# Local and strided attention scores packed into shared PSUM pairs, with batch 2's q and k transposed by DMA, in a fused attention and ELU-MLP kernel

## The chip, the cores and the metric

The kernel runs on one core of one Trainium2 chip. The metric is the device time of one execution in microseconds. TensorE (PE) multiplies, ScalarE (ACT) and VectorE (DVE) work element by element, GpSimd (POOL) here makes masks and issues most loads, and SyncE (SP) issues output stores and DMA transposes.

## The reference

Eight batches of eight heads, sequences of 576 tokens, head size 64. In heads 0 to 3 a query sees the last 32 keys (local); in heads 4 to 7 it sees earlier keys with the same position modulo 32 (strided). The result, with the heads side by side, goes through an MLP with ELU.

```python
scores = scale * np.matmul(q, k.transpose(0, 1, 3, 2))
rel = pos[:, None] - pos[None, :]
mask_local = (rel >= 0) & (rel < stride)
mask_strided = (rel >= 0) & (pos[None, :] % stride == pos[:, None] % stride)
...
attn = np.exp(scores)
attn = attn / (np.sum(attn, axis=-1, keepdims=True) + 1e-09)
return np.matmul(attn, v).astype(np.float32)
...
x = np.ascontiguousarray(attn_out.transpose(0, 2, 1, 3)).reshape(B * S, H * D)   # 4608 x 512
h = x @ w_in                                                                      # 2048 wide
g = np.where(h > 0.0, h, alpha * (np.exp(np.minimum(h, 0.0)) - 1.0))
return (g @ w_out).astype(np.float32)
```

## The kernel before, in words

Everything is one stream of tokens in the string `ORDER`, written out beforehand. The loop at the end of the kernel splits each token at its dots and calls one function; each engine then executes its instructions in the order in which the tokens issued them. A token's last field is the PSUM bank, or the banks, that it writes; there are eight banks, held as one tile `ps`, and 128 partitions.

Tokens are stored with the sequence split modulo 8 (`NS`): 72 (`RS`) positions in each of 8 residues. A strided score block is 72 by 72, because keys and queries of one residue modulo 8 meet; its mask `mask_s` does the rest. A local block takes 128 keys and 96 queries. A pair such as `2s0` or `2l1` means batch 2, strided or local heads, half 0 or 1: two heads. Each pair is worked in two units, 0 and 1.

For a batch the steps are:

- `D` loads q, k, v (`qs`, `ks`, `vs` strided; `ql`, `kl`, `vl` local), `w_in` (`wi`, `wj`) and `w_out` (`wo`). All of these are issued by GpSimd, which converts to bf16 on the way. `X` is a DMA transpose from a raw tile into `qT` or `kT`, issued by SyncE. Batches below `NPE` (3 before: batches 0, 1 and 2) have no `X`; they are transposed by TensorE with `T` (lines 418 and 421) and copied out of PSUM with `c` (VectorE) or `C` (ScalarE). For these batches `ql` and `kl` are loaded as runs of 512 bf16 columns; from `NPE` on in four loads of 64-column pieces, one for each head (L238, L245), with a second small load for `vl` (L257).
- `S` makes scores (L464): a strided unit is eight matmuls of 64 x 128 on 72 columns, a local unit six on 96 columns. Two heads are stored in two banks, 288 (`W`) columns in each. `e` is the exp on ScalarE (L471), `m` the mask product on VectorE (L478 strided, L484 local).
- `O` multiplies by the values (L527, L534; in batches 0 and 1, `OLDPV`, L491 to L512), with the sums of the softmax as extra columns. `n` takes the logarithm of the sums and `r` the exp of its negative on ScalarE (L562, L568); `x` writes the normalized result into `xT` on VectorE (L593).
- `W` and `V` copy v into its padded form on VectorE.

The MLP runs over nine chunks of 512 tokens. `L` (or, in chunk 0, `a` for two of the four row blocks and `b` for the others) is one of 16 hidden tiles: four matmuls of 128 x 128 on 512 columns (L623). `h` is the exp on ScalarE (L631), `i` a clamp on VectorE (L640) or `j` the same on ScalarE (L638), `g` the maximum with the tile in PSUM on VectorE (L651, L649). `Z` is a quarter of an output tile: four matmuls (L657). `o` (ScalarE) or `q` (VectorE) copies an output tile out of PSUM (L663), `t` stores it through SyncE's queue (L675). A chunk can start only when all batches that its 512 tokens touch are written into `xT`. The last output tile is made in two halves (`Y`, `y`).

Before `ORDER` starts, the program issues batch 0's q and k for the first strided heads through SyncE's and ScalarE's queues, then fills constants and issues the other loads of batch 0 on GpSimd. Raw tiles for q, k and v exist once (batch 1 uses free room in `xT` and `g`), so a load for a later batch waits until the transposes of the batch before have read the tile.

Of the kernel before, what the change touches and what calls it, by code (L numbers as in the profile page):

```python
# [9 lines left out]
BF16 = mybir.dt.bfloat16  # L10
I32 = mybir.dt.int32
ALU = mybir.AluOpType
# [3 lines left out]
S = 576  # L16
# [14 lines left out]
NPE = 3  # L31
OLDPV = (0, 1)


ORDER = """
w.7.28 F.k1 F.vs k.k.0 k.q.0 T.0s0.k.0.0 F.ms C.0s0.k.0 T.0s0.q.1.0 K.q.1 k.k.1 c.0s0.q.0
T.0s0.k.0.1 S.0s0.0.12 c.0s0.k.1 T.0s0.q.3.1 e.0s0.0 c.0s0.q.1 S.0s0.1.67 m.0s0.0 T.0s1.q.0 e.0s0.1
O.0s0.0.12 c.0s1.q m.0s0.1 T.0s1.k.7 n.0s0.0 F.ml D.wi0.0 O.0s0.1.56 r.0s0.0 c.0s1.k x.0s0.0 D.wj0.0
n.0s0.1 S.0s1.0.34 r.0s0.1 T.0l0.q.7 D.wi1.0 e.0s1.0 x.0s0.1 S.0s1.1.01 c.0l0.q T.0l0.k.2 e.0s1.1
D.wi2.0 m.0s1.0 c.0l0.k O.0s1.0.67 D.wi3.0 m.0s1.1 n.0s1.0 S.0l0.0.01 S.0l0.1.23 D.qs.1 V.0.0  # L40
e.0l0.0 O.0s1.1.45 e.0l0.1 D.ks.1 m.0l0.0 T.0l1.k.0 r.0s1.0 m.0l0.1 O.0l0.0.23 n.0s1.1 x.0s1.0
D.vs.1 T.0l1.q.1 r.0s1.1 c.0l1.k O.0l0.1.67 n.0l0.0 r.0l0.0 c.0l1.q n.0l0.1 V.0.1 D.ql.1 S.0l1.1.01
x.0l0.0 r.0l0.1 x.0s1.1 e.0l1.1 S.0l1.0.23 x.0l0.1 a.0.0.4 e.0l1.0 m.0l1.1 D.kl.1 O.0l1.1.67 m.0l1.0
O.0l1.0.23 n.0l1.1 r.0l1.1 a.0.2.5 n.0l1.0 x.0l1.1 a.0.1.0 r.0l1.0 D.vl.1 x.0l1.0 a.0.4.6 b.0.4
b.0.0 h.0.4 b.0.2 h.0.0 i.0.4 a.0.5.7 D.wo0.0 h.0.2 a.0.6.3 i.0.0 g.0.4 b.0.6 j.0.2 b.0.5 g.0.0
h.0.6 a.0.11.6 h.0.5 g.0.2 b.0.11 j.0.6 a.0.8.4 i.0.5 D.wo1.0 h.0.11 b.0.1 g.0.5 a.0.9.5 h.0.1 g.0.6
b.0.8 j.0.11 D.wo2.0 i.0.1 b.0.9 h.0.8 g.0.1 a.0.7.7 h.0.9 a.0.14.3 i.0.8 T.1s0.q.0 g.0.11 j.0.9
D.wo3.0 b.0.7 g.0.8 T.1s1.q.2 h.0.7 a.0.3.6 c.1s1.q T.1s0.k.1 C.1s0.q a.0.15.4 g.0.9 D.qs.2 C.1s0.k
T.1s1.k.2 i.0.7 b.0.15 c.1s1.k S.1s0.1.01 h.0.15 g.0.7 b.0.3 D.ks.2 e.1s0.1 b.0.14 i.0.15 h.0.3
g.0.15 T.1l1.q.7 S.1s0.0.01 h.0.14 m.1s0.1 S.1s1.0.45 D.ql.2 e.1s0.0 i.0.3 a.0.12.2 i.0.14 b.0.12  # L50
e.1s1.0 m.1s0.0 T.1l0.q.0 g.0.14 h.0.12 T.1l0.k.1 O.1s0.0.45 D.kl.2 C.1l0.q m.1s1.0 a.0.10.3 i.0.12
n.1s0.0 g.0.3 T.1l1.k.0 r.1s0.0 b.0.10 C.1l1.k x.1s0.0 a.0.13.6 g.0.12 h.0.10 O.1s0.1.45 C.1l0.k
c.1l1.q b.0.13 D.vs.2 V.1 n.1s0.1 S.1l1.0.12 h.0.13 Z.0.2.0.7 i.0.10 e.1l1.0 g.0.10 Z.0.1.0.0
r.1s0.1 m.1l1.0 j.0.13 x.1s0.1 S.1l0.1.12 g.0.13 O.1l1.0.34 D.vl.2 e.1l0.1 Z.0.2.1.7 n.1l1.0 m.1l0.1
r.1l1.0 Z.0.1.1.0 x.1l1.0 S.1l0.0.12 S.1s1.1.34 S.1l1.1.56 e.1l0.0 Z.0.2.2.7 e.1l1.1 m.1l0.0
Z.0.1.2.0 e.1s1.1 m.1l1.1 O.1l1.1.56 O.1l0.0.34 n.1l1.1 O.1s1.0.12 n.1l0.0 Z.0.2.3.7 m.1s1.1 n.1s1.0
r.1l0.0 r.1l1.1 Z.0.1.3.0 x.1l0.0 o.0.2 x.1l1.1 r.1s1.0 Z.0.0.0.3 t.0.2 o.0.1 x.1s1.0 Z.0.0.1.3
t.0.1 Z.0.0.2.3 Z.0.0.3.3 O.1s1.1.12 o.0.0 O.1l0.1.67 n.1s1.1 T.2s1.q.0 t.0.0 T.2s1.k.3 n.1l0.1
c.2s1.q r.1s1.1 T.2l0.k.5 c.2s1.k T.2l0.q.4 r.1l0.1 T.2l1.k.0 x.1s1.1 C.2l0.k T.2l1.q.3 x.1l0.1
S.2s1.0.12 C.2l1.k W.2 T.2s0.q.5 L.1.13.6 e.2s1.0 D.qs.3 c.2s0.q C.2l1.q c.2l0.q T.2s0.k.7 m.2s1.0  # L60
L.1.6.5 h.1.13 D.ks.3 V.2 j.1.13 c.2s0.k L.1.11.4 D.vs.3 h.1.6 g.1.13 D.ql.3 S.2s0.0.23 i.1.6 h.1.11
S.2l0.1.01 L.1.10.6 g.1.6 e.2s0.0 X.qs.3 i.1.11 e.2l0.1 L.1.8.7 m.2s0.0 h.1.10 g.1.11 O.2s0.0.01
h.1.8 L.1.5.2 m.2l0.1 i.1.10 n.2s0.0 i.1.8 O.2s1.0.34 X.ks.3 Z.0.3.0.5 g.1.10 r.2s0.0 g.1.8 h.1.5
Z.0.3.1.5 x.2s0.0 n.2s1.0 L.1.4.7 r.2s1.0 i.1.5 D.kl.3 g.1.5 L.1.7.6 h.1.4 x.2s1.0 Z.0.3.2.5 h.1.7
i.1.4 L.1.1.4 i.1.7 g.1.4 L.1.0.3 g.1.7 h.1.1 i.1.1 L.1.12.7 h.1.0 g.1.1 D.vl.3 X.ql.3 L.1.2.6 i.1.0
h.1.12 g.1.0 L.1.14.4 h.1.2 i.1.12 g.1.12 j.1.2 L.1.15.3 D.qs.4 h.1.14 g.1.2 L.1.3.7 h.1.15 i.1.14
# [86 lines left out]
def kernel(  # L153
# [157 lines left out]
    load_runs("vs", 0, 0, 2)  # L311
    load_runs("qs", 0, 2, 2)
    load_runs("ks", 0, 2, 2)
    load_runs("vs", 0, 2, 2)

    two = 1.00193786621093750

# [433 lines left out]
```

## Time and profile before

| what | value |
|---|---|
| runs | 310.74, 312.59, 312.9 us; median 312.59 |
| span of the profiled execution, first to last instruction | 309.4 us |
| its own time beside the span | not on the page; only the span is |
| TensorE busy | 297.2 us, 96%, 2374 matmuls recorded |
| VectorE, ScalarE busy | 223.4 us (72%), 233.7 us (76%) |
| GpSimd busy | 74.8 us (24%) |
| mean granted TensorE clock | 0.977 |
| DMA | 36.29 MB in 96952 packets |

The busy time of TensorE is the union of its matmuls, whose ends are modelled; a matmul's record is longer than its distance to the next one, so distances are read from start to start. Some matmul records are missing, so a count in the timeline can be one or two too low.

### The profile page before, as it was taken

What the parts mean: (1) busy time and instruction counts of PE and PEld (TensorE: products, weight loads), DVE (VectorE), ACT (ScalarE), POOL (GpSimd) and SP (SyncE); (2) the same over time, 40 slices, a digit from 0 to 9 for tenths busy, and PEclk for the clock granted to TensorE, in tenths of its full rate; (3) what the DMA queues carried; (4) which work ended last, traced back from release to release, by engine and by line L of the source; (5) the groups of instructions that cost most, each with busy time, mean ns of one, the idle gap of its engine ahead of it and who ended that gap; (6) DMA issues with size and microseconds to landing.
All of it is one profiled execution on the core that took longest, in us unless ns stands there. A gap on an engine that the chain in (4) does not pass through costs nothing.

```text
span 309.4 us, 6379 instructions
## 1 busy us (share of the span) xinstructions
PE 297.2 (96%) x2374; PEld 151.6 (49%) x2412; DVE 223.4 (72%) x445; ACT 233.7 (76%) x410; POOL 74.8 (24%) x104
## 2 busy tenths in 40 slices
PE   5989999999999999999999999999999999999994
PEld 5754545544554455444544544455444544444443
DVE  6869972999669976898689679946798359990100
ACT  4769976979887899887998997879886767881211
POOL 8933310761084048003810082000000000000000
PEclk9559999999999999999999999999999999999999
DMA  8999999999999999994999589222200220002222
GB/s 161 189 206 206 195 206 213 165 133 152 151 200 161 123 201 183 106 125 87 190 155 122 119 113 159 47 67 71 68 3 0 70 68 1 0 2 57 67 79 70
DMA packets 96952, 36.29 MB, mean 117 GB/s; under 512 B 77754, under 2 KB 92442, under 8 KB 96922
## 3 DMA queue, kind: packets, MB, share of 16 engines
q0 software_dynamic: 64608, 19.40, 61.0%
q1 hardware_dynamic: 31878, 16.09, 28.9%
q10 hardware_dynamic: 436, 0.40, 0.5%
q8 instruction: 19, 0.31, 0.4%
q14 instruction: 11, 0.09, 0.1%
HBM read 39.41 MB, written 9.44 MB: 158 GB/s over the span
## 4 chain that ended last, share of the span: by engine, by line
PE 72%; DVE 15%; DMA 6%; issue 4%; ACT 2%; DVEq 0%; ACTq 0%
PE ps L657 34%; PE ps L623 27%; DVE g L651 6%; DMA vl<-in_v_dram 5%; DVE he L640 5%; PE ps L464 3%; PE ps L527 2%; PE ps L534 2%; DVE xT L593 1%; DMA g<-in_k_dram 1%; DVE g L649 1%; PE ps L683 1%; PE ps L421 1%; PE ps L418 1%; ACT he L631 1%
## 5 line engine op out<-in xcount | busy, mean ns | idle before, releaser
L623 PE MATMUL ps<-xT,w_in_sb 128*128 128x512 bf16 x560 | 129.6, 381 | 1.5 <-DVE g L651 0.4
L657 PE MATMUL ps<-w_out_sb,g 128*128 128x512 bf16 x538 | 128.9, 379 | 1.8 <-issue 1.0
L631 ACT ACTIVATE he<-ps 128x512 f32<-128x512 f32 x144 | 84.5, 594 | 23.3 <-PE ps L623 21.0
L623 PEld LDWEIGHTS <-w_in_sb 128*128 128x128 bf16 x576 | 55.1, 98 | 65.3 <-issue 2.3
L657 PEld LDWEIGHTS <-g 128*128 128x128 bf16 x560 | 50.6, 98 | 53.4
L651 DVE TENSOR_TENSOR g<-he,ps 128x512 bf16<-128x512 bf16 x112 | 74.0, 681 | 1.5
L640 DVE TENSOR_SCALAR he<-he 128x512 bf16<-128x512 f32 x112 | 46.3, 431 | 16.2 <-ACT he L631 15.7
L593 DVE TENSOR_TENSOR xT<-ps,ln 64x576 bf16<-64x576 f32 (+1 forms) x64 | 42.4, 678 | 21.6 <-ACT ln L568 21.1
L471 ACT ACTIVATE e<-ps 128x576 bf16<-128x576 f32 (+1 forms) x64 | 39.4, 646 | 5.8 <-PE ps L464 5.0
L562 ACT ACTIVATE ln<-ps 64x576 f32<-64x576 f32 (+1 forms) x64 | 36.3, 584 | 5.8 <-PE ps L527 2.6
L568 ACT ACTIVATE ln<-ln 64x576 f32<-64x576 f32 (+1 forms) x64 | 38.7, 620 | 1.4
L663 ACT COPY osb<-ps 128x512 f32<-128x512 f32 x27 | 15.8, 585 | 29.1 <-PE ps L657 26.1
L232 POOL DMA_DIRECT2D vs<-in_v_dram x8 | 5.3, 662 | 71.7 <-DVE vsp L603 69.4
L478 DVE TENSOR_TENSOR pm<-e,mask_s 72x576 bf16<-72x576 bf16 x32 | 14.4, 451 | 11.3 <-ACT e L471 10.8
L649 DVE SCALAR_TENSOR_TENSOR g<-he,ps 128x512 bf16<-128x512 bf16 x32 | 21.7, 680 | 0.6
L638 ACT ACTIVATE he<-he 128x512 bf16<-128x512 f32 x32 | 20.1, 627 | 0.7
L484 DVE TENSOR_TENSOR pm<-e,mask_l 128x576 bf16<-128x576 bf16 x32 | 14.5, 456 | 5.4 <-ACT e L471 4.4
L238 POOL DMA_DIRECT2D ql<-in_q_dram x20 | 16.3, 821 | 0.5 <-issue 0.4
L245 POOL DMA_DIRECT2D kl<-in_k_dram x20 | 15.5, 801 | 1.2 <-DMA vs<-in_v_dram 0.9
L527 PEld LDWEIGHTS <-vsp 72*128 72x128 bf16 x192 | 9.1, 98 | 5.8 <-DVE vsp L603 0.7
L700 DVE COPY osb<-ps 128x128 f32<-128x128 f32 x1 | 0.3, 291 | 15.0 <-ACT osb L699 15.0
L534 PEld LDWEIGHTS <-vl 128*128 128x128 bf16 x144 | 8.2, 97 | 4.4
(87 smaller groups left out, 176.4 us busy)
## 6 DMA issues: line engine op xcount, KB each, us to landing
out_dram<-osb SPq DMA_DIRECT2D x31, 144.0 KB
w_out_sb<-in_moe_w_out_dram POOLq DMA_DIRECT2D x4, 512.0 KB, 15.4
vl<-in_v_dram POOLq DMA_DIRECT2D x7, 288.0 KB, 6.6
qs<-in_q_dram POOLq DMA_DIRECT2D x5, 320.0 KB, 9.5
ks<-in_k_dram POOLq DMA_DIRECT2D x5, 320.0 KB, 11.2
vs<-in_v_dram POOLq DMA_DIRECT2D x5, 320.0 KB, 6.0
w_in_sb<-in_moe_w_in_dram POOLq DMA_DIRECT2D x3, 512.0 KB, 11.2
ql<-in_q_dram POOLq DMA_DIRECT2D x20, 72.0 KB, 6.9
```

Of the source, the lines that this page charges most:

```text
L238: nc.gpsimd.dma_start(out=t[0:RS, h % 2, :, h // 2, :], in_=q[b, h].rearrange("(p s) d -> p s d", s=NS))
L471: nc.scalar.activation(e[0:R], tiles.pop(("S", key, u))[0:R], ACT.Exp, scale=scale)
L562: nc.scalar.activation(t, s_ps, ACT.Ln)
L568: nc.scalar.activation(t, t, ACT.Exp, scale=-1.0)
L593: nc.vector.tensor_mul(dst, o_ps, rc)
L623: nc.tensor.matmul(tiles["h", ch, m], lhsT=w_in_sb[:, c, m * 128:(m + 1) * 128], rhs=xT[:, c, ch * CHUNK:(ch + 1) * CHUNK], start=(c == 2) ...
L631: nc.scalar.activation(e, tiles["h", i[0], i[1]], ACT.Exp)
L638: nc.scalar.activation(e1, e, ACT.Relu, bias=1.0, scale=-1.0)
L640: eng.tensor_scalar(e1, e, scalar1=1.0, scalar2=1.0, op0=ALU.min, op1=ALU.subtract)
L649: nc.vector.scalar_tensor_tensor(dst, e1, -1.0, h, op0=ALU.mult, op1=ALU.max)
L651: nc.vector.tensor_tensor(dst, e1, h, op=ALU.max)
L657: nc.tensor.matmul(ops, lhsT=g[ch % 2][:, m, kk * 128:(kk + 1) * 128], rhs=w_out_sb[:, m, :], start=(m == 0), stop=(m == MC - 1), skip_gro ...
```

## The change

Batches 2 to 7 (`PACK`) make their scores with a new token `P` in place of `S`. For each of the four combinations of half and unit, `P.b.j` puts a local unit (288 columns) and three of the four strided blocks of the same index (3 x 72) side by side into one pair of banks: 504 (`PW`) columns in each, 12 matmuls. A fifth token, `P.b.4`, gathers the four strided blocks that are left over: 288 columns, 8 matmuls. One exp and one mask product then serve the whole pair, so a batch has five of each in place of eight. The mask tile `mask_x` holds the local mask and, beside it, `mask_s` three times with zeros in the rows below 72. The value products read their blocks out of the packed tile. Local and strided scores of a batch now need the transposed q and k of both kinds.

`NPE` falls from 3 to 2: batch 2's q and k come by DMA transposes (`X`) on SyncE's queue, its `ql` and `kl` in 64-column pieces, and its `vl` with the second small load; its eight `T` and eight copies are gone.

`ORDER` is written anew as a whole, banks included. Most of batch 0's loads are tokens now; batch 1's q and k are loaded ahead of `w_in`, and seven of its eight `T` stand ahead of the first MLP token. Two output copies of chunk 0 and most in later chunks are `q` in place of `o` (23 against 8), and there are 59 `j` against 32.

```diff
-NPE = 3
+NPE = 2
 OLDPV = (0, 1)
+PACK = (2, 3, 4, 5, 6, 7)
+PW = W + 3 * RS
...
 ORDER = """
-w.7.28 F.k1 F.vs k.k.0 k.q.0 T.0s0.k.0.0 F.ms C.0s0.k.0 T.0s0.q.1.0 K.q.1 k.k.1 c.0s0.q.0
-T.0s0.k.0.1 S.0s0.0.12 c.0s0.k.1 T.0s0.q.3.1 e.0s0.0 c.0s0.q.1 S.0s0.1.67 m.0s0.0 T.0s1.q.0 e.0s0.1
-O.0s0.0.12 c.0s1.q m.0s0.1 T.0s1.k.7 n.0s0.0 F.ml D.wi0.0 O.0s0.1.56 r.0s0.0 c.0s1.k x.0s0.0 D.wj0.0
...
-S.2s1.0.12 C.2l1.k W.2 T.2s0.q.5 L.1.13.6 e.2s1.0 D.qs.3 c.2s0.q C.2l1.q c.2l0.q T.2s0.k.7 m.2s1.0
...
+F.k1 w.7.28 K.q.1 k.k.0 T.0s0.k.0.0 D.ks1.0 k.q.0 T.0s0.q.1.0 k.k.1 T.0s0.q.2.1 C.0s0.q.1
+T.0s0.k.7.1 T.0s1.k.6 D.qs1.0 F.ms c.0s0.k.0 D.ql0.0 D.vs0.0 C.0s0.k.1 T.0s1.q.0 F.m1 F.ml D.kl0.0
+S.0s0.1.23 C.0s0.q.0 C.0s1.k e.0s0.1 c.0s1.q D.vs1.0 S.0s0.0.45 S.0s1.0.01 m.0s0.1 S.0s1.1.67
...
+S.1s0.0.45 r.0l1.1 x.0l1.1 D.vs.1 T.1s1.k.7 D.wi2.0 c.1s1.k a.0.2.0 b.0.2 C.1l0.k e.1s0.0 m.1s0.0
...
+b.0.12 j.0.7 g.0.7 O.1l0.0.67 Z.0.1.0.0 X.ql.2 h.0.13 h.0.12 n.1l0.0 Z.0.0.0.4 g.0.6 Z.0.0.1.4
...
+h.1.13 h.1.3 g.1.11 g.1.0 D.kl.3 i.1.3 i.1.4 j.1.13 P.2.4.23 e.2p.4 h.1.1 h.1.9 g.1.3 j.1.9 g.1.4
+L.1.15.1 P.2.2.23 P.2.0.67 m.2p.3 h.1.12 t.0.2 Z.0.3.2.5 i.1.1 g.1.1 Z.0.3.3.5 L.1.14.4 m.2p.1
...
+    p_pm4 = ctx.enter_context(tc.tile_pool(name="p_pm4", bufs=2)) if PACK else None
...
-    mask_l = consts.tile([128, 2, NS, 3, LN], BF16, tag="mask_l", name="mask_l")
+    mask_x = consts.tile([128, 2, PW if PACK else W], BF16, tag="mask_x", name="mask_x")
+    mask_l = mask_x[:, :, 0:W].rearrange("p u (s b n) -> p u s b n", s=NS, b=3)
...
+        elif b == 0:
+            y = int(what[2])
+            if nm == "vl":
+                load_vpair(0, y)
+            else:
+                load_runs(nm, 0, 2 * y, 2)
...
-    load_runs("vs", 0, 0, 2)
-    load_runs("qs", 0, 2, 2)
-    load_runs("ks", 0, 2, 2)
-    load_runs("vs", 0, 2, 2)
...
-    for y in range(2):
-        load_runs("ql", 0, 2 * y, 2)
-        load_runs("kl", 0, 2 * y, 2)
-        load_vpair(0, y)
...
+        elif what == "mx":
+            mx = mask_x[:, :, W:]
+            nc.vector.memset(mx, 0.0)
+            for u in range(2):
+                nc.vector.tensor_copy(mx[0:RS, u].rearrange("p (i n) -> p i n", n=RS),
+                                      mask_s.unsqueeze(1).to_broadcast([RS, 3, RS]))
+        elif what == "m1":
+            nc.gpsimd.affine_select(
+                mask_1, mask_1, compare_op=ALU.is_ge, fill=0.0,
+                base=-1, pattern=[[-1, NS], [-NS, LN]], channel_multiplier=1)
+            nc.gpsimd.affine_select(
+                mask_1, mask_1, compare_op=ALU.is_ge, fill=0.0,
+                base=PRE, pattern=[[1, NS], [NS, LN]], channel_multiplier=-1)
...
+    def scores_packed(b, j, bk):
+        i0, i1, j = int(bk[0]), int(bk[1]), int(j)
+        sc = tiles["S", b + "p", j] = ps[:, i0:i1 + 1:i1 - i0, 0:PW if j < 4 else W]
+        items = ([("l", j // 2, j % 2, i) for i in range(3)] + [("s", j // 2, j % 2, i) for i in range(3)]
+                 if j < 4 else [("s", k // 2, k % 2, 3) for k in range(4)])
+        c0 = 0 if j == 4 else W
+        for c, y, u, i in items:
+            P = Pair(f"{b}{c}{y}")
+            for z in range(2):
+                pr = slice(z * D, (z + 1) * D)
+                if P.str:
+                    x, sp = divmod(i, 2)
+                    q0 = k0 = (P.head(x) * (NS // 2) + 2 * u + sp) * RP
+                    if P.pe:
+                        k0 = (x * (NS // 2) + 2 * u + sp) * RS
+                        q0, k0 = P.q0 + k0, P.k0 + k0
+                    rhs = P.qT[pr, q0:q0 + RS]
+                    dst = sc[:, z, c0:c0 + RS]
+                else:
+                    w = 3 * u + i
+                    k0 = P.k0 + w * LQ
+                    rhs = P.qT[pr, P.q0:P.q0 + NS * P.rp].rearrange(
+                        "c (s p) -> c s p", s=NS)[:, :, w * LN:(w + 1) * LN]
+                    dst = local_cols(sc[:, z, 0:W], i)
+                nc.tensor.matmul(dst, lhsT=P.kT[pr, k0:k0 + 128], rhs=rhs, start=True, stop=True,
+                                 skip_group_check=True)
+            if P.str:
+                c0 += RS
+
+    def exp_packed(key, j):
+        j = int(j)
+        R, n = (128, PW) if j < 4 else (RS, W)
+        e = tiles["e", key, j] = p_e.tile([128, 2, PW], BF16, tag="e", name="e")
+        nc.scalar.activation(e[0:R, :, 0:n], tiles.pop(("S", key, j))[0:R], ACT.Exp, scale=scale)
+
+    def mask_packed(key, j):
+        j = int(j)
+        e = tiles.pop(("e", key, j))
+        if j == 4:
+            pm = p_pm4.tile([RS, 2, W], BF16, tag="pm4", name="pm4")
+            nc.vector.tensor_mul(
+                pm.rearrange("p z (i n) -> p (z i) n", n=RS),
+                e[0:RS, :, 0:W].rearrange("p z (i n) -> p z i n", n=RS),
+                mask_s.unsqueeze(1).unsqueeze(1).to_broadcast([RS, 2, 4, RS]))
+        else:
+            pm = p_pm.tile([128, 2, PW], BF16, tag="pm", name="pm")
+            nc.vector.tensor_mul(pm, e, mask_x[:, j % 2].unsqueeze(1).to_broadcast([128, 2, PW]))
+        tiles["pm", key, j] = pm
+
...
     def pv(key, u, bk):
         P, u = Pair(key), int(u)
-        pm = tiles.pop(("pm", key, u))
+        if P.b in PACK:
+            k = 2 * P.y + u
+            pm, pm4 = (tiles["pm", key[0] + "p", i] for i in (k, 4)) if P.str else (
+                tiles["pm", key[0] + "p", k], None)
+            c0 = W
+        else:
+            pm, c0 = tiles.pop(("pm", key, u)), 0
+
+        def part(z, i):
+            if not P.str:
+                return local_cols(pm[:, z, 0:W], i)
+            if P.b in PACK and i == 3:
+                return pm4[:, z, k * RS:(k + 1) * RS]
+            return pm[0:RS, z, c0 + i * RS:c0 + (i + 1) * RS]
+
         if not P.old:
...
+        "P": scores_packed,
...
```

## The prediction

> **What bounds the kernel now.** I read the page first (busy time, the 40 slices), then the busy time by stage in stretches of 10 us, then TensorE's timeline, then the queues' timelines.
>
> ```profile
> span 309.4 us, 6379 instructions
> PE 297.2 (96%) x2374; PEld 151.6 (49%) x2412; DVE 223.4 (72%) x445; ACT 233.7 (76%) x410; POOL 74.8 (24%) x104
> ...
> PEclk9559999999999999999999999999999999999999
> DMA  8999999999999999994999589222200220002222
> ```
>
> TensorE is busy for 96%, and the DMA engines are full up to about half of the span. The stages say where TensorE is not full (columns: stretch, its length, then busy us and instructions of PE, PEld, DVE, ACT, POOL; granted clock; DMA share; GB/s):
>
> ```profile
> 10.00:20.00 10.00, 8.80 (x164) 6.91 (x164) 8.47 (x22) 7.77 (x18) 6.15 (x9) 0.50 1.49 197
> 20.00:30.00 10.00, 9.95 (x57) 4.63 (x53) 6.96 (x14) 8.15 (x17) 4.17 (x5) 0.90 1.24 205
> ...
> 160.00:170.00 10.00, 9.95 (x52) 4.64 (x52) 10.00 (x21) 8.19 (x15) 0.00 (x0) 1.00 1.18 130
> ```
>
> From 20 us on TensorE is busy for 9.6 to 10 of every 10 us, at full clock from about 22 us, until its last matmul ends at 305.5. So an instruction taken from TensorE behind 20 us is worth its time; work taken from ScalarE and VectorE is worth only the short waits it removes. Ahead of 20 us the bound is batch 0: its loads, its chain through ScalarE and VectorE, and a half clock. The timeline (start, us, engine, line, operation, count) gives the prices:
>
> ```profile
> 18.38 0.60 PE L623 MATMUL ps<-xT,w_in_sb 128*128 128x512 bf16 x1
> ...
> 20.44 3.75 PE L623 MATMUL ps<-xT,w_in_sb 128*128 128x512 bf16 x13
> ...
> 52.80 0.43 PE L418 MATMUL ps<-identity,qs 72*128 72x72 bf16 x8
> ...
> 54.60 0.30 PE L464 MATMUL ps<-qTs,kTs 64*128 64x72 bf16 x8
> ...
> 174.26 1.02 PE L657 MATMUL ps<-w_out_sb,g 128*128 128x512 bf16 x4
> 175.12 0.42 PE L534 MATMUL ps<-pm,vl 128*128 128x96 bf16 x6
> ...
> 177.47 1.03 PE L657 MATMUL ps<-w_out_sb,g 128*128 128x512 bf16 x4
> 178.43 0.30 PE L464 MATMUL ps<-qTl,kTl 64*128 64x96 bf16 x6
> 178.66 1.04 PE L657 MATMUL ps<-w_out_sb,g 128*128 128x512 bf16 x4
> ...
> 180.84 0.43 PE L464 MATMUL ps<-qTs,kTs 64*128 64x72 bf16 x16
> 181.10 0.29 PE L464 MATMUL ps<-qTl,kTl 64*128 64x96 bf16 x6
> ```
>
> The dense MLP stream begins at 20.44. Batch 2's transposes take 52.80 to 54.60, with two more groups behind. Four L657 matmuls take 0.86 us (174.26 to 175.12); with one score group behind them 1.19 (177.47 to 178.66): a lone group costs 0.33. In a bunch a group costs 0.13 (180.84 to 181.10 for two). So entering and leaving the score shape costs 0.20, and a group itself 0.13.
>
> **The change part by part, on TensorE.** (a) Batch 2's eight transpose groups go: six of them are the 1.80 us from 52.80 to 54.60, two of 0.26 follow: -2.3. (b) The new order puts seven of batch 1's eight groups, which stand between 29.4 and 37.3 us, ahead of the first MLP matmul: by the same timeline the eight take 2.34 us, and the one that stays 0.38: -2.0. (c) Scores: behind the start of the MLP stream the old order has 56 groups in 31 bunches, 31 x 0.20 + 56 x 0.135 = 13.8 us. The new one has 7 old groups, 24 packed ones of 12 matmuls (two groups' worth, 0.27) and 6 of 8 matmuls (0.14) in 22 bunches: 4.4 + 0.9 + 6.5 + 0.8 = 12.7. -1.1: the matmuls are the same ones, only the bunches are fewer. (d) Before the dense start the old order had done two MLP matmuls (18.38); the new one none: +0.4. Work behind the start: -5.0.
>
> **The start.** w_in's loads go behind batch 1's q and k. In the old run the first w_in piece landed at 16.2 (issued at 9.2, 7.0 later, the least of that line), the fifth at 25.3 (12.2 + 13.1): 1792 KB in 9.1 us, 197 KB per us. Four loads of 320 KB ahead of it are 6.5 us: the first piece lands at 22.7; about 0.7 us of POOL's mask work that stood before it moves earlier, so 22.0 to 22.7. The second product of the first hidden tile also waits for all of batch 0's output, which ScalarE and VectorE, with seven more copies of transposes among their work, finish at about 22 (last write of batch 0 at 22.0 before). I take a dense start at 22.3: +1.9. Nothing hides it, but transposes of batch 1 fill it, which is (b). Bounds: 21.4 to 24.
>
> **The clock.** Eight matmuls from 20.50 took 2.61 us where eight later take 1.73: 0.9 was lost to the half clock, which ended at about 22 (0.90 over 20 to 30), 1.6 us into the dense stream. The head did not lift it, though the row 10 to 20 shows TensorE busy for 8.8 of 10. If it again takes 1.6 us, the change adds nothing; if the MLP matmul at 18.38 counted too and all of the 3.6 us to 22.0 was needed, the loss is 1.8 and the change adds 0.9. I take +0.3. The Trainium skill ("TensorE: Matmul & The Clock Gate", Part 1 and the passage on transposes) says that the clock is judged over free-running windows of 3.4 us and that transposes do not count as busy. The row agrees that a head of transposes stays cold; by the page the loss would be an estimated 1.7 to 3.4 us.
>
> **ScalarE and VectorE.** The lengths come from these groups (line, shapes, count, busy, mean ns):
>
> ```profile
> L471 ACT ACTIVATE e<-ps 128x576 bf16<-128x576 f32 x32 | 20.1, 647 | 3.0 <-PE ps L464 2.5
> L562 ACT ACTIVATE ln<-ps 128x288 f32<-128x288 f32 x16 | 6.2, 411 | 2.3 <-PE ps L507 1.2 <-PE ps L491 1.1
> L484 DVE TENSOR_TENSOR pm<-e,mask_l 128x576 bf16<-128x576 bf16 x32 | 14.5, 456 | 5.4 <-ACT e L471 4.4
> ```
>
> A 576-column activation takes 647 ns, one of 288 columns 411: 0.82 ns a column, so one of 1008 takes about 1.00 us (an estimate; from no growth, 0.65, to full proportion, 1.13). Per batch eight of 0.647 (5.2 us) become four of 1.00 and one of 0.65 (4.65): -0.5, six batches -3.1. The mask goes from 8 x 0.456 to about 4 x 0.68 + 0.456 (between 0.456 and 0.80): -2.8 in all. Eight copies of batch 2's transposes go (five of about 0.45 on VectorE, three of 0.65 on ScalarE). The new order also turns 27 clamps from VectorE to ScalarE and 15 output copies the other way. With these (27 x 0.431 and 27 x 0.627, 15 output copies at 0.689 and 0.585) VectorE ends some 6 us lighter and ScalarE 3 heavier, against 309 us of which they are busy 223 and 234: both lie beside TensorE. What is left is TensorE's own short waits: adding up its instructions by the prices above from 20.44, I miss some 3.6 us against the trace, 0.9 of it the clock and 1.0 between 55 and 90 us, where batch 2's copies and masks crowd the first chunks. I take -0.8 for that stretch; bounds -1.5 and, if a longer exp or a bank freed later adds waits, +2.
>
> **Batch 2 by DMA.** q and k of batch 2 now cross SP's queue: four transposes, ahead of the first output store, each behind its load. Loads stand in POOL's queue behind w_in and half of w_out; at the pace above q lands at 43.5, the last k at 52 to 56. In the old run the transposes of batch 3, in the same crowd:
>
> ```profile
> 60.29 3.06 SPq L616 DMA_TRANSPOSE qTs<-qs  x1
> 63.52 4.35 SPq L616 DMA_TRANSPOSE kTs<-ks  x1
> ...
> 71.29 0.67 POOL L232 DMA_DIRECT2D qs<-in_q_dram  x1 [2.52 <-DMA qTs<-qs]
> 75.17 0.64 POOL L232 DMA_DIRECT2D ks<-in_k_dram  x1 [3.21 <-DMA kTs<-ks]
> ```
>
> The first is done at 71.3, 11.0 after its issue, the next 3.9 later. So: 43.5 + 11.0, and three at 3.9: 66.2 for the last. By the new order and the prices above TensorE reaches the strided scores of batch 2 (behind twelve hidden tiles of chunk 1) at about 63.5 and the first that need the local k at about 66. The cover is thus 0 us thick at that point; I take 0, bounds 0 and 7.
>
> **Sum.** -5.0 + 1.9 + 0.3 - 0.8 = -3.6 us, a span of 305.8. The page gives no time but the span for the profiled execution; the runs lie 1.3 to 3.5 above it (median 3.2), so 312.6 - 3.6 = 309.0. About 1% (3.1 us) is what a measurement of this kernel tells from no change.
>
> **Rivals.** *Late start, cold clock.* As the tail of the start's bounds: start at 23.3 (+1.0) and the half clock for a whole further stretch (+0.8 to +1.7): -3.6 + 2.2 = -1.4, 311.2. For it: 0.50 over 10 to 20 us in spite of busy 8.8. Against: the old order met the same clock. The page on the clock gate, named above, speaks for this one. *Slower: the transposed k of batch 2 comes late.* If all four take what the first pair took (14.9 us from 60.29 to 75.17 for two), the last is ready at 43.5 + 29.8 = 73.3, 7.3 us behind TensorE; the stream is in order, so everything stops, and batch 3's loads, which wait for the same raw tiles, slip too. -3.6 + 7.3 = +3.7: 316.3. It is slower from a stall of 3.6 us, by over 1% from 6.7. For it: DMA slices of 9 up to 45% of the span. Against: two transposes later in the old run, with queues empty, follow each other in 1.5 us (173.1, 174.6). *The clean case.* The start at 21.4, all short waits of 20 to 90 us gone: -6, 306.6. *Packing does nothing for the time:* (c) is worth 1.1 us only; if bunches cost less than priced, -2.5, in the second case's neighbourhood.
>
> **Chances.** Forecast 0.38 and clean case 0.10: faster by over 1%, 0.48. Late start, or packing worth nothing: 0.29, within 1%. Late transposes, with a few per cent for any other wait of the new order: 0.23. The range: 305.0, the clean case a little exceeded, to 315.5, which leaves out the worst half of the slow case. The likeliest alone: 307 to 310.5.
>
> **What would show it.** Right: no transposes from PSUM behind 25 us but one group; the dense stream from 22 to 22.7; 22 bunches of scores; 1.0 us for the packed exp and 0.68 for its mask; TensorE's last matmul near 302. Wrong: a gap on TensorE ahead of the packed scores of batch 2 ended by a DMA, a clock of 0.5 beyond 26 us, or waits of scores on ScalarE's exp.

## The result, and the profile after

The changed kernel takes 311.09 us (median of 20 runs, 309.68 to 314.96), the kernel before 311.82 (20 runs beside it). The ratio is 0.9968, 95% interval 0.9955 to 0.998: faster by 0.2 to 0.45%, so within 1%, where 309.0 us and -3.6 us had been forecast. Here and below the ratios leave out runs over 1.5% above the fastest of their kernel: one of these 20, one each in e6 and e7, six of eleven in e5. The profiled execution took 310.89 us, its span is 309.0 (309.4 before). The page:

```profile
span 309.0 us, 6099 instructions
PE 296.3 (96%) x2279; PEld 151.6 (49%) x2316; DVE 221.7 (72%) x412; ACT 234.6 (76%) x402; POOL 81.2 (26%) x111
...
PEclk9556999999999999999999999999999999999999
```

TensorE has 95 instructions fewer on the page and is busy for only 0.9 us less: what it does takes longer somewhere. PEclk is low for one slice (7.7 us) more than before. The stages, in the same columns as before the change:

```profile
10.00:20.00 10.00, 8.62 (x158) 6.60 (x152) 8.41 (x22) 8.41 (x21) 6.44 (x9) 0.50 1.47 195
20.00:30.00 10.00, 9.35 (x128) 5.50 (x131) 5.96 (x14) 6.38 (x13) 4.43 (x6) 0.60 1.37 201
...
80.00:90.00 10.00, 8.92 (x58) 4.44 (x58) 5.61 (x10) 7.18 (x12) 1.13 (x2) 1.00 1.77 183
...
160.00:170.00 10.00, 9.95 (x77) 4.85 (x77) 9.45 (x19) 9.26 (x16) 4.15 (x5) 1.00 1.34 160
```

Two rows stand out: 20 to 30, where the clock is 0.60 (0.90 before), and 80 to 90, where TensorE idles for 1.08 us. In the kernel before it was 0.11:

```profile
80.00:90.00 10.00, 9.89 (x94) 5.24 (x91) 5.81 (x11) 9.02 (x16) 3.61 (x5) 1.00 1.32 170
```

TensorE's timeline shows both places, and the packed scores of batch 2:

```profile
20.43 0.69 PE L423 MATMUL ps<-identity,xT 72*64 72x72 bf16 x16 [1.06 <-DMA xT<-in_k_dram]
...
22.96 0.66 PE L420 MATMUL ps<-identity,xT 72*128 72x72 bf16 x8
23.42 0.62 PE L687 MATMUL ps<-xT,w_in_sb 128*128 128x512 bf16 x1
...
26.09 2.79 PE L687 MATMUL ps<-xT,w_in_sb 128*128 128x512 bf16 x8
...
66.50 0.30 PE L493 MATMUL ps<-qTs,kTs 64*128 64x72 bf16 x8
...
89.47 1.89 PE L687 MATMUL ps<-xT,w_in_sb 128*128 128x512 bf16 x7 [1.02 <-DVE osb L727]
```

The MLP stream starts at 23.42, behind transposes of batch 1 that waited 1.06 us for their load. It runs at half pace: eight matmuls of 512 columns from 26.09 take 2.79 us in the record, where eight at full pace take 1.90 (e7, below); start to start they are 427 ns apart until 27.9 us and 216 ns after it. Batch 2's first packed scores come at 66.50 with no wait for a DMA. The wait at 89.47 leads to VectorE, and from there to SyncE's queue (SPq; a row of several pieces runs from the first issue to the end of the last, with the queue's waits between them):

```profile
88.73 0.69 DVE L727 COPY osb<-ps 128x512 f32<-128x512 f32 x1 [2.23 <-DMA out_dram<-osb]
```

```profile
52.06 5.86 SPq L680 DMA_TRANSPOSE kTs<-ks  x1
58.09 2.60 SPq L680 DMA_TRANSPOSE kTl<-kl  x1
...
77.00 4.76 SPq L680 DMA_TRANSPOSE qTs<-qs  x1
81.86 1.38 SPq L739 DMA_DIRECT2D out_dram<-osb  x3
83.41 2.76 SPq L680 DMA_TRANSPOSE kTl<-kl  x1
86.27 4.29 SPq L739 DMA_DIRECT2D out_dram<-osb  x7
```

An output copy wants one of four osb buffers; the store that empties it stands behind batch 3's transposes and is issued at 81.86 only. These transposes are late in their turn: the first load of batch 3 waits for a DMA transpose of batch 2, issued at 52.06, to free the raw tile.

```profile
65.24 0.66 POOL L230 DMA_DIRECT2D ks<-in_k_dram  x1 [13.42 <-DMA kTs<-ks]
```

The packed groups (by form):

```profile
L502 ACT ACTIVATE e<-ps 128x1008 bf16<-128x1008 f32 x24 | 23.4, 1015 | 2.1 <-PE ps L493 2.0
L515 DVE TENSOR_TENSOR pm<-e,mask_x 128x1008 bf16<-128x1008 bf16 x24 | 16.2, 677 | 3.0 <-ACT e L502 3.0
```

### The profile page after: what moved, and what is told of

Same layout as the page of the kernel before. It is cut to its first block, busy times and chain, and to the rows that moved or that the text cites. A ratio compares the mean times of both kernels' runs of the same rounds, so it can differ in the third digit from the quotient of the medians.

```text
span 309.0 us, 6099 instructions
## 1 busy us (share of the span) xinstructions
PE 296.3 (96%) x2279; PEld 151.6 (49%) x2316; DVE 221.7 (72%) x412; ACT 234.6 (76%) x402; POOL 81.2 (26%) x111
## 4 chain that ended last, share of the span: by engine, by line
PE 70%; DVE 9%; ACT 7%; DMA 6%; issue 3%; POOL 3%; SPq 1%; DVEq 0%; ACTq 0%
PE ps L687 33%; PE ps L721 30%; DMA xT<-in_k_dram 3%; DVE g L715 3%; ACT ln L626 3%; DMA out_dram<-osb 2%; DVE he L704 2%; PE ps L493 2%; PE ps L584 2%; PE ps L577 1%; ACT e L502 1%; DVE xT L657 1%; ACT ln L632 1%; ACT he L695 1%; DVE osb L727 1%
## 5 line engine op out<-in xcount | busy, mean ns | idle before, releaser
L657 DVE TENSOR_TENSOR xT<-ps,ln 64x576 bf16<-64x576 f32 (+1 forms) x64 | 42.9, 678 | 24.2 <-ACT ln L632 23.4
L715 DVE TENSOR_TENSOR g<-he,ps 128x512 bf16<-128x512 bf16 x85 | 57.1, 684 | 1.8
L713 DVE SCALAR_TENSOR_TENSOR g<-he,ps 128x512 bf16<-128x512 bf16 x59 | 39.2, 683 | 12.6 <-ACT he L702 12.3
L704 DVE TENSOR_SCALAR he<-he 128x512 bf16<-128x512 f32 x85 | 36.1, 434 | 14.8 <-ACT he L695 14.4
L702 ACT ACTIVATE he<-he 128x512 bf16<-128x512 f32 x59 | 36.3, 630 | 1.4 <-DVE g L715 0.5
L502 ACT ACTIVATE e<-ps 128x1008 bf16<-128x1008 f32 (+1 forms) x30 | 27.3, 941 | 3.4 <-PE ps L493 3.3
L727 DVE COPY osb<-ps 128x512 f32<-128x512 f32 x23 | 15.8, 687 | 15.5 <-PE ps L721 12.9
L515 DVE TENSOR_TENSOR pm<-e,mask_x 128x1008 bf16<-128x1008 bf16 x24 | 16.2, 677 | 3.0 <-ACT e L502 3.0
L230 POOL DMA_DIRECT2D ks<-in_k_dram x7 | 4.8, 683 | 35.0 <-DMA kTs<-ks 32.0
L522 ACT ACTIVATE e<-ps 72x576 bf16<-72x576 f32 (+1 forms) x16 | 9.9, 646 | 2.4 <-PE ps L466 2.2
L727 ACT COPY osb<-ps 128x512 f32<-128x512 f32 x12 | 7.1, 593 | 5.5 <-PE ps L721 5.4
```

What stands on the lines that cost most here:

```text
L502: nc.scalar.activation(e[0:R, :, 0:n], tiles.pop(("S", key, j))[0:R], ACT.Exp, scale=scale)
L657: nc.vector.tensor_mul(dst, o_ps, rc)
L702: nc.scalar.activation(e1, e, ACT.Relu, bias=1.0, scale=-1.0)
L704: eng.tensor_scalar(e1, e, scalar1=1.0, scalar2=1.0, op0=ALU.min, op1=ALU.subtract)
L713: nc.vector.scalar_tensor_tensor(dst, e1, -1.0, h, op0=ALU.mult, op1=ALU.max)
L715: nc.vector.tensor_tensor(dst, e1, h, op=ALU.max)
```

## The experiments

My theory from this profile: the work left TensorE as forecast, and three things gave most of it back: a start later by 1.1 us than forecast, the half pace, and the late store. The rivals: longer exp and mask, a DMA limit that only moves waits about, or work that had never been on the path. Ratios below are to the kernel before; the changed kernel's is 0.9968. Single spans are read with care: with the same order at the start, the first MLP matmul came at 22.9 to 23.4 us in the changed kernel, e1, e4, e5 and e11, and, with filling, at 22.6 to 24.1 in e7, e12 and e13.

**e1: one more osb buffer.**

```
- p_osb ... bufs=4
+ p_osb ... bufs=5
```

> Five buffers of the output tile osb instead of four, nothing else. In the changed kernel the copy of an output tile (DVE, L727) waited 2.23 us at 88.7 us for the store of an earlier tile that stands behind three DMA transposes in SyncE's queue, and the MLP matmul behind it began some 1.2 us late. Theory (the moved transposes cost a late store): that wait goes, TensorE's gap of about 1 us near 88 us goes, and the span falls by 1.0 to 1.2 us, from 309.0 to about 307.9; ratio to the kernel before 0.993. Rival (the gap is given back anyway, since a later wait ends no sooner): the gap goes and the span stays within 0.3 us, ratio 0.996 to 0.997.

Measured: ratio 0.998 (0.9955 to 1.0004), span 308.2. The gap at 88 us is gone, and TensorE waits at another place on the same queue:

```profile
113.93 0.30 PE L493 MATMUL ps<-qTs,kTs 64*128 64x72 bf16 x8 [0.84 <-DMA kTs<-ks]
```

So the cause of the gap is shown, and the rival fits the time, which can't be told from the changed kernel's: batch 4's strided k, behind nine pieces of stores in the queue, takes back 0.84 us. What is left of the lower span is an MLP start 0.54 us earlier (22.88), which the edit doesn't touch. This run also tells something of the clock record:

```profile
20.00:30.00 10.00, 9.78 (x151) 5.79 (x150) 6.51 (x15) 7.23 (x16) 3.99 (x6) 1.00 1.38 200
```

```profile
25.55 2.82 PE L687 MATMUL ps<-xT,w_in_sb 128*128 128x512 bf16 x8
```

The row says clock 1.00, and eight matmuls take 2.82 us, 427 ns apart until 27.4 us. The pace of the matmuls is what counts, not the granted clock of the row. The Trainium skill ("TensorE: Matmul & The Clock Gate", "Seeing it yourself") warns that the clock's trace events have been seen to be unreliable; this run agrees.

**e2: weights ahead of batch 1's local q, k, and TensorE's order to suit.**

```
- ... O.0l0.1.67 D.kl.1 ... T.1l1.k.1 x.0l0.0 O.0l1.1.23 D.ql.1 ... D.wj0.0 T.1l0.k.6 ... T.1l0.q.1 ... D.wi0.0 ... a.0.2.0 b.0.2 ...
+ ... D.wj0.0 O.0l0.1.67 D.wi0.0 ... O.0l1.1.23 D.kl.1 ... D.ql.1 ... a.0.2.0 b.0.2 ... T.1l1.k.1 ... T.1l0.k.2 ... T.1l0.q.1 ...
```

> The first two pieces of w_in are loaded ahead of batch 1's local k and q; the last PV group of batch 0 runs ahead of the transposes of batch 1's local k and q, and these stand behind the first MLP matmuls. All work is kept. Theory (the start is late by the order of the loads and of TensorE's stream, and the half clock lasts longer for it): the first MLP matmul moves from 23.4 to about 21.3 us, the clock is granted 3.4 us earlier (24.5 instead of 27.9 us), and the span falls by 2 to 3 us, to about 306.5; ratio 0.988 to 0.991. Rival (the loads are limited by their total amount, so what starts sooner waits later, for the local q and k of batch 1 or for the third and fourth piece of w_in): the first matmul moves but the span falls by less than 0.8 us; ratio 0.994 to 0.997.

Measured: 1.006 (1.0032 to 1.0087), span 310.8. The first MLP matmul moved to 21.86, and the time got longer:

```profile
27.39 0.45 PE L423 MATMUL ps<-identity,xT 72*64 72x72 bf16 x16 [0.36 <-DVE kTl L441]
28.39 0.30 PE L466 MATMUL ps<-qTl,kTl 64*128 64x96 bf16 x6 [0.55 <-DVE qTl L437]
29.43 1.54 PE L687 MATMUL ps<-xT,w_in_sb 128*128 128x512 bf16 x3 [0.74 <-ACT e L522]
```

TensorE now stops between transposes, scores and MLP, and three MLP matmuls at 29.43 take 1.54 us: half pace until about 33 us. My number was wrong in sign: the early start, with waits and transposes in it, lost more in waits and pace than it gained.

**e3: only TensorE's order.** The last PV group of batch 0 ahead of the transposes; the loads stay.

```
- ... T.1l1.k.1 x.0l0.0 O.0l1.1.23 ... T.1l0.k.6 ... T.1l0.q.1 c.1l0.q ... S.1s0.0.45 ...
+ ... x.0l0.0 O.0l1.1.23 ... T.1l1.k.1 c.1l1.k T.1l0.k.6 C.1s1.q T.1l0.q.1 c.1l0.q S.1s0.0.45 ...
```

> Only the order of TensorE's stream (and of the copies that belong to it) at the start: the last PV group of batch 0 ahead of the transposes of batch 1's local k and q; the loads stay. Theory (both the loads and the order make the start late): the first MLP matmul stays bound by its weights, which land at 22.8 us, and starts at 22.8 to 23.4; only the wait of its second pair for the attention output (about 0.5 to 1 us at 24.3) goes; span down by 0.5 to 1.0 us, ratio 0.993 to 0.995. Rival (the weights alone set the start): nothing moves, ratio 0.996 to 0.997. A second rival (the order alone sets it): as much as with the loads moved too, 2 us or more.

Measured: 0.9975 (0.996 to 0.9989), span 308.7: no difference that can be told. The first MLP matmul came at 24.20, with the second pair 0.85 behind it as before. That gap is one matmul at half pace whose record is missing (in e5's profile it is there, 0.41 us behind the first), not a wait for the attention output, as I had read it. The new order brought a wait of its own, so it doesn't show what the order alone is worth:

```profile
22.76 0.69 PE L423 MATMUL ps<-identity,xT 72*64 72x72 bf16 x16 [1.18 <-DVE kTl L441]
```

**e4: each packed exp and mask in two.**

```
- nc.scalar.activation(e[0:R, :, 0:n], S[0:R], ACT.Exp, scale=scale)
+ for c in (slice(0, W), slice(W, n)): nc.scalar.activation(e[0:R, :, c], S[0:R, :, c], ACT.Exp, scale=scale)
```

> Each packed exp of 1008 columns becomes two (576 and 432 columns), and each packed mask likewise; the matmuls, banks and order stay. By the rows of the changed kernel this adds about 0.25 us to ScalarE and 0.15 us to VectorE for each of 24, some 6 and 4 us in all. Theory (TensorE's work is the bound behind the start, and exp and mask lie beside it): the span rises by less than 1 us, ratio 0.996 to 1.000. Rival (the score groups wait for exp and mask, so that the long exp eats what the packing saves): the span moves by several us, up where the added time lies on the path (ratio 1.005 to 1.015), or down by over 1 us where shorter parts let PV start sooner.

Measured: 0.9995 (0.9972 to 1.0017), span 310.1; by the ratios some 0.8 us more than the changed kernel, with intervals that overlap. In the profile the place that grew is the wait at 88 us, by 0.97 (1.99 us <- DVE osb L727). So exp and mask lie beside TensorE for the most part, as the theory said: the change by several us that the rival would have brought isn't there.

**e5: five buffers, and batch 4's strided k ahead of the stores.**

```
- h.2.8 t.1.1 e.3p.2 t.1.2 ... g.2.8 X.ks.4 h.2.4
+ h.2.8 X.ks.4 t.1.1 e.3p.2 t.1.2 ... g.2.8 h.2.4
```

> Five osb buffers as before, and batch 4's strided k is transposed by DMA ahead of the stores of three output tiles in SyncE's queue instead of behind them. With five buffers alone the 1.2 us at 88 us were gone, but TensorE then waited 0.84 us at 113.9 us for that transposed k, which stood behind nine store pieces. Theory (the gain of five buffers was given back at this second place on the same queue): both gaps go, span about 1.0 us under that with five buffers alone, near 307.2, ratio 0.993 to 0.995. Rival (the queue is at its limit there, so what is moved ahead pushes a third thing late): span within 0.4 us of the run with five buffers, ratio 0.996 to 0.998.

Measured: ratio 1.0057 (1.0013 to 1.0101), but the median of all eleven runs is 316.1 us (311.4 to 319.6), some 5 us above e1's; span 313.9. The wait moved to a third place and grew:

```profile
122.76 0.42 PE L493 MATMUL ps<-qTl,kTl 64*128 64x96 bf16 x6 [5.23 <-DMA qTl<-ql]
```

The rival's kind of wait came, and larger than it had said: what is moved ahead in this queue makes a third thing late, and TensorE's in-order stream makes the delay a full stop. That the queue is full there isn't shown.

**e6: the transposes behind the first MLP matmuls, matmuls of zeros in their place.**

```
- ... T.1l1.k.1 x.0l0.0 O.0l1.1.23 ... T.1l0.k.6 ... T.1l0.q.1 ... S.1s0.0.45 ... T.1s1.k.7 ... a.0.2.0 b.0.2 ... a.0.3.3 b.0.3
+ ... x.0l0.0 O.0l1.1.23 ... w.7.30 S.1s0.0.45 ... a.0.2.0 b.0.2 T.1s1.k.7 ... T.1l0.k.2 ... a.0.3.3 b.0.3 ... T.1l1.k.1 ... T.1l0.q.1
```

> While TensorE waits for the first weights (19.4 to 22.8 us) it runs 30 matmuls of zeros (128 columns each) and one score group instead of the transposes of batch 1's local q, k, which stand behind the first MLP matmuls. These come at half pace (427 ns for 512 columns) until 27.4 to 28.1 us in all versions with this start, and at 216 ns after it. Theory (the pace rises only after some 3 to 4 us in which TensorE is filled with matmuls, and transposes do not fill it): 216 ns from 23 to 24.5 us on; this saves 1.5 to 2 us of half pace, and the transposes that now stand in the dense stream cost 1.0 to 1.3 us of it, so the span falls by 0.3 to 1.0 us, to 308.0 to 308.7, ratio 0.993 to 0.996. Rival (the pace rises at its own time, or transposes fill it as well): 427 ns until 27 us and later, span 1 us and more longer, ratio 1.000 to 1.004.

Measured: 1.0025 (0.9994 to 1.0055), span 310.8. Half of the theory: matmuls are 216 ns apart from 23.7 us on, four us earlier. But the transposes and three waits (0.49, 0.55 and 0.74 us) now lie in the stream between 24.6 and 29.6, and from 30 to 33.6 the pace is half again.

**e7: matmuls of zeros in two idle places only.**

```
- n.0l0.1 T.1l1.k.1 ... a.0.2.0 b.0.2
+ n.0l0.1 w.7.10 T.1l1.k.1 ... a.0.2.0 w.7.6 b.0.2
```

> Only the two idle places at the start are filled with matmuls of zeros: 10 in the 1.06 us before the transposes of batch 1's local k, and 6 between the first and the second pair of MLP matmuls; all else stays. Theory (what counts is the share of some 3.4 us that is filled with matmuls, and 3 us of transposes lie in between): the pace rises at most one window earlier, at about 24.5 instead of 27.9 us, if the filled 24.3 us tip it, or not at all; span 307.5 if it does (ratio 0.991 to 0.993), else within 0.4 us of the changed kernel (0.996 to 0.998). Rival (idle time alone holds the pace down, transposes count): the pace rises by 24 us, span 307.0 to 307.5.

Measured: 0.9929 (0.9894 to 0.9963), 309.68 us, 1.4 less than the changed kernel; the profiled span is 305.8.

```profile
18.82 1.25 PE L399 MATMUL ps<-zero 128*128 128x128 bf16 x10
20.00 0.66 PE L423 MATMUL ps<-identity,xT 72*64 72x72 bf16 x16
...
22.61 0.60 PE L687 MATMUL ps<-xT,w_in_sb 128*128 128x512 bf16 x2
...
24.65 1.90 PE L687 MATMUL ps<-xT,w_in_sb 128*128 128x512 bf16 x8
```

The first MLP matmuls run at full pace (two in 0.60 us, eight in 1.90). The ten zero matmuls took 1.25 us, half pace, so the pace rose about 20 us, after 3 us with nothing but matmuls in them (PV groups from 16.9, then the zeros). The transposes behind did not bring it down. So the half pace is a large part of what was given back: its removal is worth 1.4 us by the medians (the intervals of the ratios still touch), up to 2.2 by the pace. This profiled run is the fastest of eight, and in it the wait at 88 us is 0.4 us.

**e8: the kernel before, with batch 2 by DMA alone.**

```
- NPE = 3
+ NPE = 2
- T.2s1.q.0 ... c.2s0.k (eight T, eight copies, V.2)   o.0.2 x.1l1.1 r.1s1.0 Z.0.0.0.3 t.0.2
+ X.qs.2 X.ks.2 X.ql.2 X.kl.2 o.0.2 x.1l1.1 r.1s1.0 Z.0.0.0.3 t.0.2
```

> The kernel before with one part of the change alone: batch 2's q and k are transposed by DMA (four transposes ahead of the stores of three output tiles on SyncE), its eight groups of transposes on TensorE and the ten copies are left out, and its first score group stands some 2 us later. Theory (TensorE is the bound, the prediction's first term): minus 2.3 us where the DMA transposes arrive in time, ratio 0.992 to 0.994. Rival (the transposed k is late, its loads land at 48.7 and 51.9 us and its first scores stand at about 54 us): a gap of 1 to 4 us near 54 to 57 us ended by a DMA, ratio 0.997 to 1.006. Second rival (the saved time goes to a later wait for stores or for batch 3's transposes on the same queue): the gap lies behind 70 us, ratio 0.996 to 1.000.

Measured: 1.0401 (1.0371 to 1.0431), 324.59 us: 12 us slower.

```profile
56.85 2.55 SPq L616 DMA_TRANSPOSE kTl<-kl  x1
59.50 11.51 SPq L675 DMA_DIRECT2D out_dram<-osb  x8
```

```profile
70.72 0.42 PE L464 MATMUL ps<-qTl,kTl 64*128 64x96 bf16 x6 [11.12 <-DMA kTl<-kl]
```

The rival, and three times larger than I had put it. The last transpose, issued at 56.85, is done at 70.7 beside seven pieces of stores and batch 3's loads; the row's eighth piece goes out only then, at 70.69. The slower rival of the prediction is real in the old order. In the changed kernel batch 2's first scores stand later (66.5 instead of 54.6), and only three pieces of stores follow the transposes at once; which of the two keeps the stall away isn't shown.

**e9: the kernel before with its own idle places filled.**

```
- S.0l1.1.01 x.0l0.0 ... a.0.0.4 e.0l1.0 ... r.0l1.1 a.0.2.5
+ S.0l1.1.01 w.3.8 x.0l0.0 ... a.0.0.4 w.3.6 e.0l1.0 ... r.0l1.1 w.2.4 a.0.2.5
```

> The kernel before with its own idle places at the start filled: 8, 6 and 4 matmuls of zeros (128 columns) ahead of the last local score group, behind the first MLP pair and ahead of the second. In the kernel before the pace was 427 ns for 512 columns until 22.0 us, with dense MLP work from 20.44; in the changed kernel the same filling brought the full pace from 27.9 to 22.6 us at the latest and 2 us and more of time. Theory (the changed kernel loses more to the half pace than the kernel before, and this is a part of what was given back): the kernel before gains at most 0.5 to 0.9 us from filling (1.6 us of dense half pace, half of it saved), ratio 0.997 to 0.999. Rival (both lose the same): ratio 0.990 to 0.994, as with the changed kernel filled.

Measured: 1.0036 (1.0009 to 1.0063). Neither theory: filling made it slower. The zeros ran at half pace, the first eight for 1.04 us ahead of a score group that batch 0's chain was waiting for, the dense stream began at 23.5 instead of 20.4 (0.8 of it from before 10 us, where nothing was changed), and the pace still rose only at 26.1. The run says nothing on what the kernel before loses to its half pace; in these places the zeros cost more than they brought.

**e10: filling at four places, and five buffers.** As e7, with 4 zeros ahead of `O.0l0.1.67` and 6 ahead of `T.1l0.q.1`, and e1's fifth buffer.

> The changed kernel with idle places at the start filled (4, 10, 6 and 6 matmuls of zeros) and five osb buffers. Theory (half pace and the late store are two separate losses, the second partly given back at batch 4's transposed k): span 305.0 to 306.5, ratio 0.988 to 0.992. Rival (with five buffers the wait only moves, and more filling pushes the transposes late): as with the filling alone or slower, ratio 0.993 to 0.996.

Measured: 0.9917 (0.9895 to 0.9938), 309.1 us, profiled span 307.2 with the MLP start at 24.0. The interval overlaps that of e7: a gain from the buffer isn't shown.

**e11: 11 of 24 packed score groups taken apart.** (Some banks are written here before the tile in them has been read, so the scores differ from the reference; instructions and lengths are the same.)

```
- L.2.5.6 P.3.1.12
+ P.3.1.12.l L.2.5.6 P.3.1.12.s
```

> In the changed kernel 11 of the 24 packed score groups are taken apart: their local half is issued one MLP block earlier, ahead of four MLP matmuls, the strided half where the whole stood; exp, mask and banks stay. So TensorE enters score mode 11 times more, with the same matmuls. Theory (the prediction's price: 0.20 us for each entry, which is what packing saves): 11 times 0.20, span up by 2.2 us, to 311.2 (with up to 1 us more where the banks are not free that early); ratio 1.004 to 1.008. Rival (the entries cost nothing, the score matmuls hide behind the weights): ratio 0.996 to 0.998.

Measured: 1.0215 (1.0186 to 1.0244), 318.17 us, 7 more than the changed kernel. Between MLP blocks a lone local half costs 0.33 us and a whole one 0.43 (medians of the time from the last MLP matmul before to the first behind, less one matmul), a lone strided half 0.30, so a split costs 0.33 + 0.30 - 0.43 = 0.20: 2.2 us for 11. The price of an entry, 0.20, was good. Of the rest the profile shows waits, the longest 2.26 us at 217 us; that the earlier use of banks brought them about is likely, but no run shows it.

**e12 and e13: filling (as e7) with five buffers, and the same with batch 2's transposes back on TensorE.** For e13:

```
- NPE = 2 ... X.qs.2 X.ql.2 X.ks.2 X.kl.2
+ NPE = 3 ... Z.0.1.3.0 T.2s0.q.1 c.2s0.q ... Z.0.0.2.4 T.2s1.q.2 C.2s1.q L.1.7.7 T.2s0.k.1 c.2s0.k ... (eight T, eight copies)
```

> The changed kernel with 10 and 6 matmuls of zeros in the two idle places at the start, and five osb buffers; 10 filling matmuls fewer than in the run before it, which began its dense work 1.4 us later than the one with filling alone. Theory (dense start near 22.6 us at full pace, no late store at 88 us): span 305 to 306.5, ratio 0.985 to 0.990. Rival (the start is set by when the loads happen to land, the filling costs nothing): as the run before it, 307, ratio 0.991 to 0.993.

> The same with one part of the change undone: batch 2's q and k are transposed on TensorE again (eight groups between MLP blocks at 51 to 58 us, through banks that are free there, with eight copies on VectorE and ScalarE), the four DMA transposes are left out, batch 3's load of strided k stands three MLP blocks later. Theory (the prediction's first term): TensorE gets 8 times 0.26 us and the changes of mode, so 2.3 to 3.0 us slower than the kernel beside it; ratio of this to it 1.007 to 1.010. Rival (the DMA transposes of batch 2 cost as much elsewhere, by holding stores and batch 3's transposes on the queue): within 0.8 us of it, or faster.

Measured: e12 0.991 (0.9884 to 0.9935), 308.99 us, profiled span 305.9: faster than both kernels, not told apart from e7 and e10. Against e1 (0.998, 0.9955 to 1.0004) it differs by the filling alone, and these intervals lie apart: filling is worth 0.7%, some 2 us. e13 1.0024 (0.9999 to 1.0048), 312.3 us: 3.3 us slower than e12. In e13's profile the eight groups stand between MLP blocks and one wait comes with them:

```profile
59.06 0.71 PE L423 MATMUL ps<-identity,kl 72*64 72x72 bf16 x32
60.96 1.24 PE L687 MATMUL ps<-xT,w_in_sb 128*128 128x512 bf16 x5 [1.19 <-DVE g L715]
```

Eight groups at 0.26 with their changes of mode are 2.4 us, the wait 1.2; of the 5.2 us between the two spans, 1.3 are a later MLP start (24.10 against 22.82), which the edit doesn't touch. So the largest term of the sum is real in the changed order, at 2.4 to 3.3 us, though alone in the kernel before the same part costs 12 us.

## Why the prediction was wrong

The direction was right, the amount was not: -0.4 us of span against -3.6 (-0.7 by the medians), so 3.2 us are to be found. Starts, stretches and waits below are those of the two profiled executions.

- **(a) batch 2's transposes, -2.3:** right. e13 puts it at 3.3 us by the medians, with a wait of 1.2 in its profile.
- **(b) batch 1's transposes ahead of the stream, -2.0:** they left the dense stream, as the timeline from 20.43 to 22.96 shows; not tested by itself, and what they did to the start is below.
- **(c) scores, -1.1:** right in price (0.33 and 0.43 in the trace, 0.20 for a split in e11) and in the number of bunches, 31 before and 22 after. Behind 60 us the stretches between MLP blocks with scores in them sum to 13.1 us before (24 of them) and 11.6 after (18), by the same count as in e11: -1.5.
- **"The start", +1.9:** measured +3.0 (23.42 against 20.44), 1.1 too little. The failed step is where the stream was taken to begin as soon as weights and batch 0's output were there, at 22.3; the first weights landed at 22.82. Ahead of the first MLP matmul in TensorE's order stand transposes of batch 1's local k, whose load landed only at 20.39, and four groups more at half pace. Batch 0's last output was written only by 23.5, not at about 22, but the second pair of matmuls, at 24.26, shows no wait for it. In e2 loads and order together bring the start to 21.86 but not the time, and in e3 another order brings no earlier start; so what the start alone is worth isn't shown.
- **"The clock", +0.3:** the stream ran at half pace for 4.5 us (23.42 to 27.9), a loss of 2.2 us, against 0.8 to 0.9 before: +1.3 to 1.4. The failed step is the choice of a row (1.6 us into the stream, as in the kernel before) over the estimated loss of 1.7 to 3.4 us that it had worked out from the Trainium skill. That text ("TensorE: Matmul & The Clock Gate", Part 4) says that transposes do not count as busy in the same way as matmuls; here the pace rose 4.5 us after the last transposes, in a stretch where TensorE had hardly been idle since 20.43. That agrees with it and is not a proof of it. The rival "late start, cold clock" named the right mechanism. That its 311.2 us lies so near 311.09 is in part luck: it was counted from the 312.6 of three runs, where 20 runs give 311.82, and as a difference it was -1.4 us against -0.7; it also lacks the store.
- **"Batch 2 by DMA", 0:** for batch 2's own scores the answer holds, no wait at 66.5. The failed step is that the queue was followed only as far as batch 2's own scores. Behind them on SyncE stand batch 3's transposes and the stores, and a store late by its place in this queue stops TensorE for 1.02 us at 88 us. That batch 2's DMA transposes make it late is borne out by e13, which has none: this second store of the queue is issued at 72.70, against 79.57 in e12 (lines of e12, then of e13, below). In e1 and e5 one buffer and one move don't mend it: the wait goes to 114 and to 123 us.

```profile
79.57 1.37 SPq L739 DMA_DIRECT2D out_dram<-osb  x3
...
72.70 1.38 SPq L739 DMA_DIRECT2D out_dram<-osb  x3
```

- **"ScalarE and VectorE", -0.8:** exp 1015 ns and mask 677, as estimated; e4 shows that they lie beside TensorE. Short waits from 50 to 90 us: TensorE's idle time in the four stage rows was 0.77 us before; after, it is 1.39 with the 1.02 above and 0.37 without: -0.4, half of what I took.

In sum: 1.1 (start) + 1.0 (clock) + 1.0 (store) + 0.4 (waits) = 3.5, less the 0.4 by which (c) came out better: 3.1 of the 3.2 that were missing. "TensorE's last matmul near 302" failed with them: it ends at 305.1.

That this sum closes so well is luck in part, since its first three terms move from one execution to the next. e8 has the old order at the start: its dense stream begins at 21.08 (20.44 above) and stays at half pace for 2.7 us (1.6 above). The two part early: four transposes at 5.5 us take 0.30 us in the profile before and 0.42 in e8.

```profile
5.50 0.30 PE L418 MATMUL ps<-identity,ks 72*128 72x72 bf16 x4 [1.27 <-ACT ks L402]
...
5.54 0.42 PE L418 MATMUL ps<-identity,ks 72*128 72x72 bf16 x4 [1.32 <-ACT ks L402]
...
21.08 3.22 PE L623 MATMUL ps<-xT,w_in_sb 128*128 128x512 bf16 x8
```

With the changed kernel's order the start lies between 22.9 and 23.4, and the half pace ends 2.3 us after it in e11 (below) and 4.9 us after it in e4.

```profile
25.87 1.90 PE L678 MATMUL ps<-xT,w_in_sb 128*128 128x512 bf16 x8
```

So, by these profiles, the start is +1.8 to +3.0 and the clock -0.2 to +1.6; the wait for the store is 0.4 (e7) to 2.0 us (e4) where there are four buffers. What is firm: each of the six profiles with the late start and no filling (changed kernel, e1, e3, e4, e5, e11) has its first MLP matmuls at half pace, each of the four with filling there (e7, e10, e12, e13) at full pace, and filling brings back about 2 us. What stays open is the size of each term in the medians, and why the fifth buffer, whose effect on the gap is plain, shows no gain there.

## What to carry to other kernels

Follow a transfer queue past the work that you moved to the next thing that stands in it, here a store, and from there to the buffer that it frees. Price the start of a dense stream at the pace the engine will have there, by what precedes it; a few matmuls of zeros in an idle place, ahead of the stream, bought more time (1.4 us here, by the medians) than the change itself (0.7). And a part of a change can be worth +3 us in one order and -12 in another, so its price belongs to the order and not to the part.

## What the runs showed of the hardware

- The granted clock of the record and the pace of the matmuls can differ: clock 1.00 in e1's row, 427 ns for 512 columns until 27.4 us.
- A DMA transpose of a raw tile took 14 us from its issue (56.85 to 70.7, e8) with seven store pieces and the next batch's loads behind it; the eighth store piece was issued only at 70.69, so the row of 11.51 us is for the most part a wait.
- The moment at which the pace rises moves between executions with the same start: 2.3 us (e11) to 4.9 us (e4) after the first MLP matmul.
- Full pace, once reached, can go again within 10 us: in e6 from 23.7 to 30, with transposes and waits of 0.5 to 0.7 us in between, and half pace from there to 33.6.
